# Chunk 0 of a DeltaNet layer in two halves of 32 tokens, in front of an MLP that fills TensorE

## The chip, the cores and the metric

The kernel runs on one core of one Trainium2 chip. The metric is the time of one execution on the device, in microseconds. TensorE (PE) multiplies matrices, VectorE (DVE), ScalarE (ACT) and GpSimd (POOL) do the elementwise work, and SyncE (SP) issues DMAs; ACT and POOL issue DMAs too. Everything is in 32-bit floats.

## The reference

Two layers, one after the other. The first is a DeltaNet recurrence for 4 batches, 8 heads, 768 tokens and a head size of 48; the second a layer norm and an MLP with a residual, on rows of 384.

```python
k_n = k / (np.linalg.norm(k, axis=-1, keepdims=True) + 1e-06)
for t in range(S):
    kt, vt, bt = (k_n[:, :, t], v[:, :, t], beta[:, :, t, None])
    y[:, :, t] = np.einsum('bhd,bhde->bhe', q[:, :, t], state)
    v_old = np.einsum('bhde,bhd->bhe', state, kt)
    state = state + bt[:, :, :, None] * np.einsum('bhd,bhe->bhde', kt, vt - v_old)
...
x = y.transpose(0, 2, 1, 3).reshape(B, S, H * D)
xn = (x - mu) / np.sqrt(var + 1e-06) * g_ln
out = x + np.maximum(xn @ w_ch1, 0.0) @ w_ch2
```

## The kernel before

**Chunks.** The 768 tokens are cut into 12 chunks of 64. Inside a chunk the recurrence becomes products of small matrices: the Gram matrix G of the keys, its scaled lower triangle, the inverse of one plus that triangle (one 64x64 matrix for each of the 32 batch and head pairs), u (the corrected values, from the inverse and v), the masked products P of queries and keys, the outputs y = P u plus the queries on the state, and the state's update. Then each chunk's 256 rows (4 batches of 64 tokens) go through the layer norm and the MLP.

**Three ways to the inverse.** Chunk 0 has nothing ahead of it, so its inverse is on the way of everything. It is made by doubling blocks, in `first_inverse` (line 648): at level n blocks of 2^n rows are joined. Each level has a product E (line 722), a predicated copy under a mask (731), a product Z (741), transposes on DVE (687) that give the natural form, and copies on ACT (681) that give the turned form. Chunk 0 needs five levels of products after a beginning, for two groups `g` of 8 heads each; a product is 16 matrix products of 64x64, in four quarters of the array, and each is two PE instructions. Chunks 1 to 11 use `rows_inverse` (826): the Gram matrix goes to DRAM and comes back with one 32x32 block in each partition, and DVE eliminates row by row, 31 steps of a multiplication (860) and a subtraction (867). The result is stored, loaded into `xt`, and `join` (883) joins two blocks of 32 into 64. The first call, ri1 below, is for chunk 1 alone, the second, ri2, for chunks 2 and 3, the third, ri4, for chunks 4 and 5.

**Chunk 0's rows.** Partitions hold a pair of batches of 64 tokens each (`half(e)`), and the second pair lies beside it. `first_beta` turns beta on PE, `first_norms` takes the norms of the keys, `first_swaps` moves the norms to the other half of the partitions, and `recur(0, ...)` makes u, y, the layer norm and the state. MLP 0 is done by halves of 128 rows in `by_halves` (1317): w1 in 12 blocks f (1326), relu on ACT (1334), w2 in 12 blocks (1341). The later MLPs run in blocks of 256 rows (1300) or in forms with fewer products (1221, 1423).

**Weights.** The MLP's weights come in 12 pieces of 768 KB, 0 to 5 for w1 and 6 to 11 for w2. Each is fetched by a DMA on ACT's queue into one of five buffers (`fetch`), converted by two steps on ACT (524, 532) and one on DVE (529), and added on POOL (542). A buffer is free for the next piece when its sum is done.

**Order.** All work is put down as steps by `add`; the numbers in `ORDER` then say in which order they are given out. Each engine does its own steps in exactly that order (`in_this_order`), so a step that waits holds back all later steps of its engine, DMA issues on its queue included. "z" in the list is a product of zeros on PE. The arguments `due`, `t0`, `pr`, `cap` and the costs have no effect: `Line.add` drops them.

Of the kernel before, what the change touches and what calls it, by code (L numbers as in the profile page):

```python
# [63 lines left out]
155 243 148 238 151 236 332 152 225 675 156 z 215 157 240 159 158 214 237 239 160 216 162 161 257 46 241 168 164 166 333 206 165 334 245 207 417 163  # L64
# [136 lines left out]
def kernel(  # L201
# [240 lines left out]
    def nat(src, c, e):  # L442
        return src[2 * e : 2 * e + 2, :, c * C : (c + 1) * C, :].rearrange("g h p d -> p (g h) d")
# [1209 lines left out]
```

## Time and profile before

| | |
|---|---|
| time, median of 3 runs | 507.94 us (506.93 to 510.24) |
| span of the profiled execution | 508.8 us; its own time is not listed apart from it |
| PE busy | 488.6 us, 96% |
| DVE, ACT, POOL busy | 353.8, 249.0, 275.6 us |
| first product of MLP 0 | 54.46 us |
| mean granted clock of PE | 0.965 |

The span runs from the first to the last instruction. A line of the timeline has the start, the time that a run of like instructions took, the engine, the line of the kernel, what was written from what, partitions and elements, and how many; in brackets stands how long the engine was idle just before, and what ended that. "Issue" there means that the engine waited for nothing that the profile shows. A granted clock of 0.50 means that PE ran at half speed.

### The profile page before, as it was taken

The numbers are of one execution on the slowest core, as the hardware profiler recorded it, in microseconds if no ns is written. First come the engines' busy times: TensorE is split into PE (matmuls) and PEld (weight loads), VectorE is DVE, ScalarE is ACT, GpSimd is POOL, SyncE is SP. The second block draws the span as 40 slices with busy tenths as digits, with TensorE's granted clock in tenths as the row PEclk, the third lists the DMA queues.
The fourth block names the chain that finished last, engine by engine and source line by source line (L and its number), as shares of the span: only waits on it lengthen the run. The fifth ranks groups of instructions, "written<-read, shape, count | busy, mean of one in ns | idle before, by whom it ended". The sixth has DMA issues, their size and how long they took to land.

```text
span 508.8 us, 22190 instructions
## 1 busy us (share of the span) xinstructions
PE 488.6 (96%) x9606; PEld 447.6 (88%) x9606; DVE 353.8 (70%) x780; ACT 249.0 (49%) x620; POOL 275.6 (54%) x430
## 2 busy tenths in 40 slices
PE   7778999999899999999999999999999999999996
PEld 3667988788788898899999999999999999999996
DVE  9668987997679648896649898568899328143251
ACT  5758873643544524627435535435563257363230
POOL 5464537264755496438894363492543850645633
PEclk9756799999999999999999999999999999999999
DMA  8988796667656566546834434766154402211101
GB/s 168 293 160 190 249 200 85 98 152 130 90 86 87 187 119 119 65 99 149 194 58 62 94 62 135 150 94 97 50 92 106 111 20 45 60 48 46 24 18 31
DMA packets 196097, 54.99 MB, mean 108 GB/s; under 512 B 186076, under 2 KB 189404, under 8 KB 196000
## 3 DMA queue, kind: packets, MB, share of 16 engines
q1 hardware_dynamic: 189920, 40.58, 41.9%
q10 hardware_dynamic: 3872, 9.83, 6.0%
q0 software_dynamic: 2208, 3.17, 3.8%
q8 instruction: 75, 1.23, 1.0%
q14 instruction: 22, 0.18, 0.1%
HBM read 36.64 MB, written 16.91 MB: 105 GB/s over the span
## 4 chain that ended last, share of the span: by engine, by line
PE 90%; DVE 5%; issue 2%; POOL 1%; DMA 1%; SPq 0%; ACT 0%; DVEq 0%; POOLq 0%; ACTq 0%
PE f L1423 29%; PE f L1221 22%; PE f L1300 9%; PE f L1326 4%; PE f L1341 3%; PE by L983 2%; PE by L1024 2%; PE two L983 2%; PE by L775 2%; PE two L1017 2%; PE two L775 2%; PE two L1034 2%; PE f L775 1%; DMA xt<-xd 1%; PE by L741 1%
## 5 line engine op out<-in xcount | busy, mean ns | idle before, releaser
L1410 POOL TENSOR_TENSOR h_all<-h_all 128x256 f32<-128x256 f32 x123 | 89.9, 742 | 135.1 <-PE f L1423 121.3
L1423 PE MATMUL f<-w_sb,h_all 128*128 128x192 f32 x492 | 109.8, 332 | 1.6 <-DVE rstd L967 1.6
L1423 PEld LDWEIGHTS f<-w_sb,h_all 128*128 128x128 f32 x492 | 81.8, 190 | 3.6 <-issue 1.9
L1423 PE MATMUL f<-words,h_all 128*128 128x192 f32 x396 | 84.5, 330 | 0.3 <-POOL h_all L1410 0.3
L860 DVE TENSOR_TENSOR tmp<-xb,gb 128x87 f32<-128x87 f32 (+21 forms) x186 | 73.7, 396 | 4.9
L867 DVE TENSOR_TENSOR xb<-xb,tmp 128x87 f32<-128x87 f32 (+21 forms) x186 | 73.6, 396 | 4.8
L1241 DVE TENSOR_TENSOR h_all<-h_all,f 128x512 f32<-128x512 f32 x96 | 63.5, 682 | 14.3 <-PE f L1221 13.2
L1423 PEld LDWEIGHTS f<-words,h_all 128*128 128x128 f32 x396 | 66.6, 190 | 1.7 <-POOL h_all L1410 1.0
L1300 PE MATMUL f<-xnt,w_sb 128*128 128x256 f32 x216 | 50.2, 382 | 0.0
L349 POOL DMA_DIRECT2D tb<-in_k_dram x64 | 42.0, 660 | 10.3 <-DVE kt L755 9.4
L1243 ACT ACTIVATE h_all<-h_all 128x512 f32<-128x512 f32 x48 | 28.5, 624 | 34.6 <-DVE h_all L1241 34.3
L1300 PEld LDWEIGHTS f<-xnt,w_sb 128*128 128x128 f32 x216 | 40.2, 190 | 5.3
L1237 ACT COPY h_all<-f 128x512 f32<-128x512 f32 x48 | 26.2, 590 | 34.3 <-PE f L1221 17.4
L1441 DVE TENSOR_TENSOR o<-f,x 128x192 f32<-128x192 f32 x33 | 11.6, 352 | 38.9 <-PE f L1423 22.3
L1221 PE MATMUL f<-words,w_sb 128*128 128x128 f32 x256 | 31.7, 276 | 0.0
L1309 ACT ACTIVATE h_all<-f 128x256 f32<-128x256 f32 x36 | 13.3, 382 | 35.1 <-PE f L1300 34.9
L1221 PEld LDWEIGHTS f<-words,w_sb 128*128 128x128 f32 x256 | 30.0, 192 | 0.2
L1221 PE MATMUL f<-xnt,w_sb 128*128 128x128 f32 x192 | 25.4, 276 | 0.0
L542 POOL TENSOR_TENSOR w_sb<-words 128x768 uint32<-128x768 uint32 (+1 forms) x11 | 15.0, 1365 | 17.7 <-DVE words L529 13.3
L1221 PEld LDWEIGHTS f<-xnt,w_sb 128*128 128x128 f32 x192 | 23.7, 192 | 0.1
L1326 PEld LDWEIGHTS f<-xnt,w_sb 128*128 128x128 f32 x144 | 19.2, 200 | 3.3 <-issue 0.2
L1088 ACT ACTIVATE xnt<-xnt,g_sb 128x256 f32<-128x256 f32 x27 | 12.5, 498 | 19.2 <-DMA xnt<-xld 19.1
(246 smaller groups left out, 958.4 us busy)
## 6 DMA issues: line engine op xcount, KB each, us to landing
words<-in_moe_w_ch_dram ACTq DMA_DIRECT2D x10, 768.0 KB, 5.2
gd<-gsb SPq DMA_DIRECT2D x11, 512.0 KB, 3.6
v<-in_v_dram SPq DMA_DIRECT2D x24, 192.0 KB, 4.3
kr<-in_k_dram SPq DMA_DIRECT2D x46, 96.0 KB, 3.6
out_dram<-o SPq DMA_DIRECT2D x44, 96.0 KB, 2.8
xld<-xlt SPq DMA_DIRECT2D x9, 384.0 KB, 3.3
xnt<-xld SPq DMA_DIRECT2D x36, 96.0 KB, 3.2
gb<-gd SPq DMA_DIRECT2D x44, 64.0 KB, 3.0
```

Of the source, the lines that this page charges most:

```text
L349: add(eng, cost, lambda: QUEUE[eng].dma_start(out=out_, in_=in_), r, w, bulk=n * ns / 16e3, **kw)
L775: nc.tensor.matmul(pair[hp][half(e ^ (hp & n)), (g * NP + j) * C : (g * NP + j + 1) * C], kt[drows(hp), l], rt[drows(hp), i],)
L860: lambda j=j, n=n, w=w, t=t: nc.vector.tensor_tensor(out=t, in0=xv[:, 0:n, j : j + 1].to_broadcast([np_, n, w]), in1=gv[:, j : j + 1, j + ...
L867: "DVE", dve(n * w), lambda t=t, rest=rest: nc.vector.tensor_tensor(out=rest, in0=rest, in1=t, op=ALU.subtract),
L1221: nc.tensor.matmul(wide(p[:, 128 * n : 128 * n + 128]), w[n // 2][:, n % 2 * 128 : n % 2 * 128 + 128], r, start=start and n == 0, stop=Tru ...
L1237: add("ACT", act(512), lambda: nc.scalar.copy(o, p), pk, ok)
L1241: add("DVE", dve(512), lambda: nc.vector.tensor_tensor(out=o, in0=o, in1=p, op=op), pk, ok)
L1243: add("ACT", act(512), lambda: nc.scalar.activation(o, o, ACTF.Relu), [], ok)
L1300: nc.tensor.matmul(p[:, 0:TOK], w1_sb[:, t, f * 128 : (f + 1) * 128], xnt[:, t], start=(t == 0), stop=(t == KC - 1))
L1326: nc.tensor.matmul(p[:, 0:128], w1_sb[:, t, f * 128 : (f + 1) * 128], xnt[:, t, cols], start=(t == 0), stop=(t == KC - 1))
L1410: add(eng, cost, lambda: e.tensor_tensor(out=out_, in0=x, in1=y, op=op), r, w, port=2 if eng == "Pool" else 1, pr=-2)
L1423: lambda f=f, t=start and f == 0: nc.tensor.matmul(p[:, 0:D2], lhs(f), rhs[:, f], start=t, stop=(f == F2 - 1), skip_group_check=True),
```

## The change

Chunk 0 is cut into two halves of 32 tokens. Half `g` holds tokens 32g to 32g + 31 of all four batches, with 32 partitions for each batch (`quad(b)`) and the heads side by side. Chunk 1 and all later ones are computed as before.

- The loads of k, q and v for chunk 0 become eight of 32 tokens each (`load_first`), k on SP and ACT, q and v on SP; beta comes in four rows of loads, and DVE turns it (`btok`). `first_swaps` is gone.
- `first_inverse(g, ...)` makes the 32x32 inverses of one half, in four levels. The scaled Gram matrices of two batches are set beside zeros as blocks of 64, so that E and Z are each 8 products of 128x64 by 64 columns. The turned form is brought back by four copies on ACT, the natural form by two transposes on DVE.
- Half 0 goes through u, y and the layer norm by itself. For half 1, `first_between` keeps the products of its keys with half 0's; they take half 0's u off the values (w0), and its y has a term from each half (y0x, y0).
- The state after chunk 0 is made in two parts (`first_state`), with two products for each block, one from each half.
- In the MLP by halves, a half is now 32 tokens of four batches; its outputs are stored by four DMAs for each half, for two before.
- Masks and begin matrices are fewer and lie in other tiles.
- `ORDER` is new from end to end: 3016 steps for 2997, and two "z" for one.

The core of the diff, without the order:

```diff
+    def load_first(src, dst, keys, engs, g, **kw):
+        for b in range(4):
+            dma(
+                engs[b % len(engs)], dst[quad(b), g * H : g * H + H, 0:D],
+                src[b, :, g * BK : g * BK + BK, :].rearrange("h t d -> t h d"), H * BK, 16.5, [], keys(b, g), **kw,
+            )
...
+    def first_beta(**kw):
+        add("DVE", 0.23, lambda: nc.vector.transpose(btok, brow), [("brow", b) for b in range(4)] + ["brow0"], ["btok"], **kw)
...
+    def first_between(pair, **kw):
+        for hp in range(2):
+            v, dst = parts_of(pair, hp, 0)[:, :, 1], pts[0][:, hp : H : 2]
...
+    def first_inverse(g, pair, E, Z, **kw):
...
+        for n in range(1, LAST + 1):
...
+            def prod_e():
                 for j in range(NP):
+                    for hp in range(2):
+                        nc.tensor.matmul(
+                            ebank[half(hp), j * C : j * C + C], gs[:, 2 * j + hp], xn[:, 2 * j + hp].rearrange("p e t -> p (e t)")
+                        )
+            pe(16, prod_e, [("g", 0, g), ("qt", 1, g, 0), ("qt", 1, g, 1)], ek, 0.43, name=f"E{n}{g}", **kw)
...
+            def prod_z(ep=ep):
+                for j in range(NP):
+                    for e in range(2):
                         nc.tensor.matmul(
+                            zbank[half(e), j * C : j * C + C], ep[:, 2 * j + e], xt[:, j, e].rearrange("p n t -> p (n t)")
                         )
+            pe(16, prod_z, [ekey, *xtk], zk, 0.43, name=f"Z{n}{g}", **kw)
+            z = heads_of(zbank)
+            if n < LAST:
+                nat(z, zk)
+                back(z, zk, n)
+            else:
+                add("ACT", act(256), lambda: nc.scalar.copy(done, z), zk, [("done", g)], **kw)
...
+        def first_u(g, ps, pk):
+            xd, p_u = dones[:, heads2[g]], ps[:, 0:DM].rearrange("p (h d) -> p h d", d=D)
+
+            def prod_u():
+                for h in range(H):
+                    for b in range(4):
+                        nc.tensor.matmul(p_u[quad(b), h], xd[quad(b), h], vv[quad(b), g * H + h])
...
+        if not c:
+            for g in range(2):
...
+                if g:
+                    p_w = first_half(0, pu, uk, [(pts[0][:, 0:H], 0)], [("pt", 0, 0), ("u", 0)], "w0")
...
+                first_u(g, pu, uk)
+                if g:
+                    first_half(0, py, yk, [(pts[1][:, H:GH], 0)], [("pt", 1, 1), ("u", 0)], "y0x")
+                first_half(g, py, yk, [(pts[1 - g][:, heads2[g]], g)], [("pt", 1 - g, g), ("u", g)], f"y0{g}")
...
+                ln_act(0, x, kw, (g,))
+                turn_x(g, pu, uk)
+            for b in range(2):
+                first_state(b)
+            return
...
-            for e in range(2):
+            for b in range(4) if not c else ():
+                dma("SP", out[b, g * BK : g * BK + BK], os_[g][quad(b)], BK, 105, o_keys(g), [("out", c, g, b)], pr=-5)
```

What each engine does, in the new order, around the start of MLP 0 (names as above; "f" and "w2" are the MLP's blocks):

- PE: E3 and Z3 of half 0, then Z1 of half 1, E4 of half 0, P of half 0, E2 of half 1, Z4 of half 0, Z2 of half 1, u of half 0, E3 of half 1, y of half 0, Z3 of half 1, P of half 1, the transpose of half 0's rows, E4 of half 1, f0, f1, w0, Z4 of half 1, f2, a transpose for chunk 2's keys, f4, the other one, u of half 1, f6, f3, f8, y0x, y0, G of chunk 2, ... the join of chunk 1 follows block 5 of half 1's w2.
- DVE: the last predicated copy of half 1, a mask of P, and only then ri1's 31 row steps, with the conversions of pieces 6 to 8 and 11 and half 1's steps among them. Before, ri1 began between levels 3 and 4.
- ACT: the scalings of half 0's rows, a conversion step of piece 6, the first relu, the other step of piece 6, the fetch of piece 8, a step of piece 7, the next two relus.
- SP: k, then chunk 1's k, q and v of chunk 0, chunk 1's Gram matrix out and back. Later: two reads for ri2, ri1's result out, six more reads for ri2, one load of q, then the four loads of ri1's result.

More of the change, by code (lines that the diff above doesn't have):

```diff
@@ L389 @@
     )
-    MASKED = (0, 1, 2, 3, 4, 5)
+    MASKED = (0, 1, 2, 3, 4)
     for n in MASKED:
@@ L453, in load_v @@
         for e in range(2):
-            dma("SP", vs[c % NV][half(e)], nat(v, c, e), GH * C, 16.5, w=[("v", c % NV, e)], **kw)
+            dma(
+                "SP", vs[c % NV][half(e)], nat(v, c, e), GH * C, 16.5, w=[("v", c % NV, e)],
+                after=[("v", 0, 2 * e + b, g) for b in range(2) for g in range(2)] if c == 2 else (), **kw,
+            )
     def load_raw(c, engs=("SP", "SP"), dst=None, keys=None, **kw):
@@ L618, in scale_v, with first_v @@
+    def first_v(g, **kw):
+        vg, kg = vs[0][:, heads2[g]], knrm[0][:, heads2[g], None].to_broadcast([128, H, D])
+        add(
+            "Pool", 0.8, lambda: nc.gpsimd.tensor_tensor(out=vg, in0=vg, in1=kg, op=ALU.mult),
+            [("kn", 0, g)], [("v", 0, b, g) for b in range(4)], **kw,
+        )
     def scale_v(c, kn, kk, **kw):
@@ new lines, in parts_of, with first_p @@
+    def parts_of(pair, hp, g):
+        return pair[hp][:, 0 : NP * C * (2 - g)].rearrange("p (j g t) -> p j g t", j=NP, t=C)
+    def first_p(g, pair, **kw):
+        first_products(qts[0], "qt", g, pair, f"P0{g}", **kw)
+        for hp in range(2):
+            v, dst = parts_of(pair, hp, g), pts[1 - g].rearrange("p (g j n) t -> p g j n t", g=2, n=2)[:, g:, :, hp].rearrange("p g j t -> p j g t")
+            mask = both[:, None, 0 : 2 - g].to_broadcast([128, NP, 2 - g, C])
+            add(
+                "DVE", dve(256 * (2 - g)), lambda v=v, dst=dst, mask=mask: nc.vector.tensor_tensor(out=dst, in0=v, in1=mask, op=ALU.mult),
+                pair[2 + hp] + ["own", "pown"], [("pt", 1 - g, n) for n in range(g, 2)], **kw,
+            )
@@ L706, in first_inverse @@
                 ),
-                [("g", 0, g), ("mask", 0)], bk, port=1, **kw,
+                [*ek, ("mask", n)], [ekey], **kw,
             )
-            add(
-                "DVE", dve(512), lambda i=i: nc.vector.transpose(xnj_[:, :, i], begin[:, :, i]), bk,
-                [("qt", 1, g, n) for n in range(2)], **kw,
-            )
-            back(g, lambda n, r, i=i: begin[r, n, i], [bk, bk])
-        for n in range(1, 6):
-            ep, ekey = paired(BEGIN[n][0]), tuple(BEGIN[n][1:])
-            for g in range(2):
-                E, i = next(turns), half_g[g]
-                def prod_e(i=i, E=E, n=n):
-                    for j, hp, e in order:
-                        a = half(e ^ hp)
+            def prod_z(ep=ep):
+                for j in range(NP):
+                    for e in range(2):
@@ L809, in queries @@
                 ),
-                pk + ["pmask"], [("pt", one_of(c))], after=[("pt", 1, g) for g in range(2)] if c == 1 else (), **kw,
+                pk + ["pmask"], [("pt", one_of(c))], after=[("pt", one_of(c), g) for g in range(2)] if c < 3 else (), **kw,
             )
@@ L918, in join, with raw_keys0 @@
             )
+    def raw_keys0(g):
+        return [("kr", 0, b, g) for b in range(4)] + [("krpad", 0)]
     def raw_keys(c):
@@ L937, in norms, with ln_act @@
         scale_v(c, knrm[i], kk, **kw)
-    def ln_act(c, x, kw):
+    def ln_act(c, x, kw, parts=(0, 1)):
         i = c % 2
-        for g in range(2):
+        for g in parts:
             ck = [("ln", i, g)]
@@ L969, in ln_act @@
                 add("ACT", act(384), lambda g=g, rs=rs: nc.scalar.mul(xlns[g], xlns[g], rs), ck, [("xln", g)], **kw)
+    SK = [("s_all", b) for b in range(2)]
     def recur(c, pr, lag=0.0):
@@ new lines, in first_half, with prod @@
+        def first_half(g, ps, pk, terms, keys, name):
+            p_ = ps[:, 0:DM].rearrange("p (h d) -> p h d", d=D)
+            def prod():
+                for n, (lhs, g0) in enumerate(terms):
+                    for h in range(H):
+                        for e in range(2):
+                            nc.tensor.matmul(
+                                p_[half(e), h], lhs[half(e), h], us[half(e), g0 * H + h],
+                                start=(g == 0 and n == 0 and h == 0), stop=(g == 1 or n == len(terms) - 1), skip_group_check=True,
+                            )
+            pe(32 * len(terms), prod, keys, pk, 0.64 * len(terms), name=name, **kp_e)
+            return p_
@@ L1019, in recur, with turn_x, turn, out_y @@
             add("ACT", act(768), lambda: nc.scalar.copy(u_j, p_2), TWO, [("u", 0), ("u", 1)], **kw)
-        def out_y(js, p_y=p_y):
-            for j in js:
+        xnt = xnts[c % 2]
+        unbegun = [("begin", g) for g in range(2)] if c == 1 else ()
+        def turn_x(g, tp=None, bk=None):
+            tp, bk = (by[:, g], BY[2 * g : 2 * g + 2]) if c else (tp, bk)
+            def turn():
+                for t in range(KC):
+                    nc.tensor.transpose(tp[:, t * 128 : (t + 1) * 128], xlns[g][:, t * 128 : (t + 1) * 128], ident)
+            add("PE", 0.33, turn, [("xln", g), "ident"], bk, np=3, arr=0.33, **kp_e)
+            if g > c:
+                add(
+                    "DVE", dve(384),
+                    lambda: nc.vector.tensor_tensor(
+                        out=xnt[:, :, g * 128 : (g + 1) * 128], in0=tp[:, 0:DM].rearrange("p (t n) -> p t n", t=KC),
+                        in1=g_sb[:, :, None].to_broadcast([128, KC, 128]), op=ALU.mult,
+                    ),
+                    bk + ["g_sb"], [("xnt", c % 2, g, t) for t in range(KC)], after=unbegun, **kw,
+                )
+                return
+            for t in range(KC):
+                add(
+                    "ACT", act(128),
+                    lambda t=t: nc.scalar.mul(
+                        xnt[:, t, g * 128 : (g + 1) * 128], tp[:, t * 128 : (t + 1) * 128], g_sb[:, t : t + 1]
+                    ),
+                    bk + ["g_sb"], [("xnt", c % 2, g, t)], after=unbegun, **kw,
+                )
+        def out_y():
+            for j in range(GP):
                 for hp, e in hp_e:
+                    a = half(e ^ hp)
                     nc.tensor.matmul(
-                        p_y[half(e), hp, j], pt[half(e ^ hp), 2 * j + hp], us[half(e ^ hp), 2 * j + hp],
-                        start=(c == 0 and j == js[0]), stop=True, skip_group_check=True,
+                        p_y[half(e), hp, j], pt[a, 2 * j + hp], us[a, 2 * j + hp], start=False, stop=True, skip_group_check=True,
                     )
@@ L1036, in state_up, with first_state, prod_s @@
                     )
+        def first_state(b):
+            ps, pk = ((p_2, TWO), (p_y, BY))[b]
+            def prod_s():
+                for j in range(NP):
+                    for hp, e in hp_e:
+                        a = quad(2 * e + b)
+                        for g in range(2):
+                            h0 = g * H + 2 * j + hp
+                            nc.tensor.matmul(
+                                ps[DP * hp : DP * hp + DP, e, j], kp[a, h0 * DP : h0 * DP + DP], us[a, h0],
+                                start=(g == 0), stop=(g == 1), skip_group_check=True,
+                            )
+            rk = raw_keys0(0) + raw_keys0(1)
+            add("PE", 0.8, prod_s, rk + [("u", 0), ("u", 1)], pk, np=64, arr=0.32, name=f"s0{b}", pr=-40, lag=lag)
+            add(
+                "ACT", act(384), lambda: nc.scalar.copy(s_all[:, :, b * NP : b * NP + NP], ps[:, :, 0:NP]), pk, [("s_all", b)], pr=-40,
+            )
         def up(**kw):
@@ new lines, in up, with y_copy @@
+            add("DVE", dve(768), lambda: nc.vector.tensor_tensor(out=s_all, in0=s_all, in1=p_2, op=ALU.add), TWO, SK, **kw)
+        y_j = x.rearrange("p g (j n d) -> p g n j d", n=2, d=D)
+        def y_copy(g):
+            add(
+                "ACT", act(384), lambda: nc.scalar.activation(
+                    y_j[:, g], p_y[:, :, g * NP : g * NP + NP], ACTF.Copy, accum_out=st[:, c % 2, g, 0:1]
+                ),
+                BY, [("x", c % 2, g), ("ln", c % 2, g)], **kw,
+            )
@@ L1152, in sums_of_w1 @@
     def sums_of_w1(last):
-        gone = [(n, 1, *x) for n in ("qt", "pt") for x in ((), *((g, *y) for g in range(2) for y in ((), (0,), (1,))))]
+        gone = [("done", g) for g in range(2)] + [(n, 1, *x) for n in ("qt", "pt") for x in ((), *((g, *y) for g in range(2) for y in ((), (0,), (1,))))]
         sub, plus, both = ALU.subtract, ALU.add, (0, 1)
@@ L1353, in by_halves @@
                 pk + [("x", 0, g), ("ln", 0, g)], o_keys(g), pr=-5,
+                after=["nought", "xor", "bits", "eye", *[("mask", n) for n in MASKED]],
             )
@@ L1495 @@
     chain = dict(pr=-100)
-    load_raw(0, ("SP", "ACT"), **chain)
+    add("Pool", 0.1, lambda: nc.gpsimd.memset(brow, 0.0), [], ["brow0"], pr=-100)
+    raw0 = kraws[0].rearrange("p (h d) -> p h d", d=DP)
+    load_first(k, raw0, lambda b, g: [("kr", 0, b, g)], ("SP", "ACT"), 0, **chain)
+    for b in range(4):
+        dma("Pool", brow[BK * b : BK * b + H], beta[b, :, 0:C], H, 20, ["brow0"], [("brow", b)], **chain)
+    load_first(k, raw0, lambda b, g: [("kr", 0, b, g)], ("SP", "ACT"), 1, **chain)
     load_raw(1, pr=-100)
```

402 lines of the change are left out of this document (179 added, 223 removed), and 167 rows, old and new, of the table ORDER.

## The prediction

> **What bounds the kernel now.** I read the page's totals first, then the busy time by stretches, then the first 130 us engine by engine, with what each waited for.
>
> ```profile
> span 508.8 us, 22190 instructions
> PE 488.6 (96%) x9606; PEld 447.6 (88%) x9606; DVE 353.8 (70%) x780; ACT 249.0 (49%) x620; POOL 275.6 (54%) x430
> ```
> TensorE is busy for all but 20.2 us. The stretches (PE, PEld, DVE, ACT, POOL, then granted clock, DMA share, GB/s) show where:
>
> ```profile
> 10.00:20.00 10.00, 6.94 (x203) 5.84 (x202) 7.36 (x20) 7.91 (x21) 0.90 (x2) 0.77 1.11 305
> 30.00:40.00 10.00, 7.48 (x213) 6.44 (x211) 5.88 (x21) 4.69 (x14) 4.98 (x6) 0.50 0.82 152
> 60.00:70.00 10.00, 9.91 (x209) 8.77 (x201) 9.35 (x23) 6.95 (x19) 4.54 (x6) 1.00 0.94 239
> 110.00:120.00 10.00, 10.00 (x103) 8.63 (x106) 9.40 (x20) 2.34 (x7) 4.70 (x7) 1.00 0.35 96
> 120.00:140.00 20.00, 18.28 (x349) 16.28 (x342) 11.88 (x23) 9.70 (x30) 13.95 (x21) 1.00 0.74 98
> ```
> Up to 50 us PE idles about 13 us and runs at half clock. From 54 us it is full, but for some 2.5 us between 137 and 144 and the last tail. So only what moves the start of the saturated part, adds PE work behind it, or makes new stalls there can move the end. DVE is over 90% full from 60 to 120 us: the row inverses of chunk 1 (ri1) and of chunks 2 and 3 (ri2). The marks of this part in the PE timeline:
>
> ```profile
> 13.46 0.69 PE L722 MATMUL two<-qt,gsb 64*64 64x64 f32 x32 [0.18 <-DVE qt L710]
> 18.90 1.97 PE L568 MATMUL f<-ident,tb 128*128 128x128 f32 x8
> 32.06 1.08 PE L722 MATMUL by<-qt,gsb 64*64 64x32 f32 x32
> 36.20 0.59 PE L741 MATMUL by<-xt,xt 64*64 64x64 f32 x11 [1.53 <-issue]
> 46.37 1.65 PE L1000 MATMUL two<-v,xt 64*64 64x48 f32 x32
> 54.46 2.52 PE L1326 MATMUL f<-xnt,w_sb 128*128 128x128 f32 x12
> 86.19 0.75 PE L898 MATMUL f<-xnj,gsb 32*32 32x32 f32 x64
> 104.48 2.75 PE L1300 MATMUL f<-xnt,w_sb 128*128 128x256 f32 x12
> 124.90 0.75 PE L898 MATMUL f<-xnj,gsb 32*32 32x32 f32 x64
> ```
> In order: level 1 of chunk 0's inverse, a transpose at half clock, level 4, u of the first half (46.37), the start of MLP 0 (54.46), join of chunk 1 (86.19), MLP 1 (104.48), join of chunk 2 (124.90). I call the start of MLP 0 **T**.
>
> **Part 1: the start of chunk 0.** The order lists were read by numbering the add calls; each engine's sequence follows. On POOL four beta rows replace two, and the fourth stands behind a 0.95 us clear, two half clears, the identity, g_sb and one k block. By rows (DMA issue 0.62 to 0.72, clear 0.95) it is issued near 7.9 us and lands 3.4 later (median of the beta loads), at 11.3. Behind the DVE instruction that waits for it are queued the scale, both halves of the scaled Gram matrix, the masked begin and its transposes: ten small ones at 0.15 to 0.23, two of 0.40, two of 0.45, two of 0.43, 4.4 us. Level 1 begins near 15.8, not 13.46: **+2.3**. One k load sits behind an ACT copy and lands near 8, in that cover. The sixteen q and v loads on SP (0.63 each, 10 us) replace four of 3.6 us together; SP waited 8.2 us there for the Gram copy, which hides them.
>
> **Part 2: four levels for five.** Before, five levels with both groups took 13.46 to 46.1, 6.5 each. Now half 0 goes ahead and half 1 trails. A product is 16 instructions of 64 columns on 128x64 tiles, a shape the trace lacks. Bounds: 0.69 us (32 of 64x64 at full clock) and 1.97 (eight transposes of 128 columns at half clock, if the two column halves don't overlap). I take 1.05: two halves of 16 have the columns of four quarters of 32, and those took 1.08 at half clock. A level is then E 1.05, predicated copy 0.71, Z 1.05, two transposes 0.86, some 0.4 of handovers: 4.1. Following the new lists, level 3 waits about 1.9 us for four ACT copies that stand behind weight conversions of 0.55 each, and level 4 waits 2.8 us on PE for P of half 0 (32 of 128 columns, 1.75) and E2 of half 1. Four levels: 20.7, so 36.5, against 46.1.
>
> **Part 3: from the inverse to T.** Copy of the finished inverse 0.4, then Z2 of half 1 on PE, u at 37.5. From u to T took 54.46 - 46.37 = 8.1. The chain is the same (u, scale, y, copy, mean, centre, transpose, three scalings); four products of half 1 fill the gaps that the last Z and G2 filled. T = 45.6, **8.9 earlier**. Doubt: the four PE gaps marked "issue" before (5.1 us together) may come three times; but I priced PE at half clock throughout, where two stretches ran at full. I give T 40 to 51.
>
> **Part 4: PE work that now lies behind T.** At full clock, per instruction 0.017 (64 in 1.08): correction of half 1 (w0, 32) 0.54; last Z of half 1 0.45; kt2 transposes 0.9; u of half 1 (64) 1.08; y of half 1 in two terms 1.08 against 0.65; G2 1.09; the state in two parts of 64 for one of 64, +1.08. Sum **+5.6**. Before, u of half 1, kt2 and G2 lay ahead of or at T. Were PE alone the limit, the end would move -8.9 + 5.6 = -3.3.
> A change of tile size costs: in the saturated part an interval of 0.33 grows to 0.42 ahead of the 32x32 products at 187 us, and the next group takes 0.59, not 0.49. That is 0.1 each way; six more changes, +0.6. The Trainium skill, TensorEngine Tiling (Array Packing), section Key Properties, says that changing the tiling mode drains TensorE; the row agrees and sets its size.
>
> **Part 5: what is late next.** The old list starts ri1's 62 steps at 41.8, inside the inverse's waits:
>
> ```profile
> 41.81 0.14 DVE L860 TENSOR_TENSOR tmp<-xb,gb 64x31 f32<-64x31 f32 x1
> 73.80 0.51 SPq L349 DMA_DIRECT2D xd<-xb  x1
> 78.46 2.08 SPq L349 DMA_DIRECT2D xt<-xd  x4
> 85.35 0.70 DVE L888 STREAM_TRANSPOSE xnj<-xt 128x512 f32<-128x512 f32 x1
> ```
> The new list puts them behind half 1's last predicated copy, at T + 1. They took 24.1 us (L860 12.91 + L867 11.20); 4.9 of other steps lie among them (four conversions at 0.55, w0's subtraction, u, centre, xnt, mask). End: T + 30 = 75.6, later than the 72.5 of before. Then store, six reads of ri2 and one q load on SP at 0.6, loads, landings, ri2's scaling, transpose: 13.7 us before (72.5 to 86.2). Two reads already stand ahead of the store now; I take 11.5: join 1 at T + 41.5 = 87.1. PE's own list reaches it after 37.2 us of work, at 82.8 to 84. So it stalls 3 to 4 us, and the gain of part 4 is gone.
> From join 1 the chain to MLP 1 is 16.2 (e to z 2.4, to u 2.4, to y 2.2, y 1.1, norm 5.5, transpose and scale 2.6) over 13.6 us of PE work. MLP 1: 87.1 + 16.2 = 103.3, with G5 (1.1) still to do: 104.4 against 104.48, -0.1.
> ri2 starts at T + 40.5 and has 22.9 of its own and 9.8 of others among it (6.5 before), 33.5 with gaps: 119.6 against 115.3. Store to join 2 took 9.6: 129.2, with 3.3 us more products done than at 124.9: +1.0. Before lost 2.4 near 138 to 144 (1.6 at DVE rstd, 0.8 at issue); the new list's join 3 stands about 1.3 short: -1.1. The eight output stores of chunk 0 (four before, 0.5 each) are +2 us on SP, partly ahead of ri2's loads; its cover is this stall, and I charge nothing. From 160 us on the PE work is the same, and PE has no idle time there.
>
> **Sum.** -0.1 + 1.1 - 1.1 is -0.1; the 0.6 of tile changes falls into the stalls ahead of the joins. The span stays 508.8 - 0.1 = 508.7. The runs shown have median 507.94, 0.9 below that span, so the time is **508 us**. Its own bounds come from T (-4.5 to +4.5 around 45.6) and 2 for the stalls: 503 to 513.
>
> **Rivals.**
> (a) *The start comes earlier and everything follows.* The PE clock was 1.00 from 22.5 to 25.5 and from 43.5 to 45. If it stays so through the inverse, eight products save 0.4 each, P 0.9, u 0.6, two products of half 1 0.8: 5.5 us, T = 40, end 502.5; with join 1's data 1.5 sooner, 501. For it: less queued on DVE, and fewer issue gaps. Against it: PE has 256 product instructions for 640, so it is idle more, and with 640 it already ran at 0.50 from 30 to 42. The Trainium skill, TensorE: Matmul & The Clock Gate, Terms and Part 1, says an idle window of about 3.4 us halves the clock; the rows agree in direction, and by it this rival is the less likely.
> (b) *The first relu waits for weights; slower.* ACT's new list has the conversion of piece 6 ahead of the first relu and piece 7 ahead of the second. Piece 6 can be fetched only when piece 3 has been added by POOL (near 35). Fetches land in 5.2 us at the median: 41, in time. But DMA was 0.82 to 1.11 busy in these stretches, and T's 8.9 us ask for the same bytes sooner. From a landing after 46 each microsecond stops the two relu banks, PE behind them, and on DVE ri1 behind the conversion of piece 6. A landing in 11 to 12 us adds 6: 514.
> (c) *The 128x64 products cost twice; slower.* At the upper bound 1.97, eight on the chain of half 0 add 7.4, and part is hidden by conversions: T near 52, end 514.5. For it: no row shows the shape. Against it: the 64x64 quarters do overlap.
> (d) *PE alone limits.* If ri1 and its loads keep up, -3.3 + 0.6: 505. MLP by halves exists already, so the words of the change promise nothing more there.
>
> **How the numbers follow.** Forecast 0.34, (d) 0.08, (a) 0.27, (b) 0.17, (c) 0.14. A measurement of this kernel tells about 1%, 5 us, from no change. (a) is faster by over 1%; forecast and (d) are within, less 0.01 on the slow edge; (b) and (c) are over it. So 0.27 faster, 0.41 same, 0.32 slower. The range reaches to (a) and past (b) and (c) by their 2 us: 500 to 517; the likeliest case's own is 503 to 513.
>
> **What would show it.** Right: level 1 near 16, four levels of 4 to 6 us, MLP 0 from 43 to 48, ri1 ending later than 72 us, a PE wait of 2 to 5 us ahead of the join of chunk 1, and MLP 1 near 104. Wrong: MLP 0 by 41 (a); PE waiting on ACT relu behind a words DMA after T (b); products of 1.9 us (c); no wait at join 1 (d). A forecast within 1% that comes from T at 45.6 with losses elsewhere than at join 1 would be right by accident.

## The result, and the profile after

The changed kernel takes 536.69 us (median of 4 runs, 534.01 to 538.66), the kernel before, measured beside it, 507.84: a ratio of 1.0554, 95% interval 1.0514 to 1.0594. The forecast was 508, its range 500 to 517; the kernel got 28.9 us slower. The times and ratios of the experiments below come from four chips, on each of which the kernel before took 507.6 to 509.4 us beside them. The page's totals of the kernel after:

```profile
span 534.5 us, 21792 instructions
...
PE 500.2 (94%) x9408; PEld 451.6 (84%) x9408; DVE 361.6 (68%) x778; ACT 248.6 (47%) x616; POOL 277.6 (52%) x438
```

PE idles 34.3 us instead of 20.2, and it is busy for 11.6 us more. The stretches of the kernel after (PE, PEld, DVE, ACT, POOL, then granted clock, DMA share, GB/s) show both:

```profile
20.00:40.00 20.00, 11.71 (x234) 9.42 (x228) 10.93 (x28) 15.52 (x41) 11.74 (x19) 0.80 0.57 167
...
50.00:60.00 10.00, 3.45 (x41) 3.01 (x32) 6.83 (x17) 3.15 (x10) 1.47 (x1) 0.80 0.80 159
...
60.00:80.00 20.00, 18.44 (x389) 16.84 (x388) 14.53 (x33) 12.78 (x31) 7.00 (x7) 0.93 0.59 173
...
100.00:120.00 20.00, 17.21 (x424) 12.90 (x425) 17.13 (x43) 10.13 (x31) 9.56 (x15) 0.91 0.62 83
...
120.00:140.00 20.00, 19.34 (x269) 16.37 (x268) 17.23 (x42) 7.54 (x21) 6.79 (x12) 1.00 0.49 124
```

From 50 to 60 us, where MLP 0 was to be under way, PE works 3.45 us of 10. The same marks in the PE timeline as before the change:

```profile
18.90 0.69 PE L737 MATMUL f<-qt,gsb 128*64 128x64 f32 x16
...
40.57 1.07 PE L754 MATMUL f<-xt,xt 128*64 128x64 f32 x16
...
43.09 1.50 PE L1017 MATMUL f<-v,q_last 32*32 32x48 f32 x64
...
50.08 0.55 PE L1058 MATMUL f<-ident,xln 128*128 128x128 f32 x3
...
57.87 2.93 PE L1392 MATMUL f<-xnt,w_sb 128*128 128x128 f32 x12 [6.37 <-ACT xnt L1073]
...
104.60 0.75 PE L911 MATMUL f<-xnj,gsb 32*32 32x32 f32 x64 [0.36 <-DVE xnj L901]
...
123.36 1.56 PE L1366 MATMUL f<-xnt,w_sb 128*128 128x256 f32 x6 [0.66 <-ACT xnt L1073]
...
148.77 0.75 PE L911 MATMUL f<-xnj,gsb 32*32 32x32 f32 x64
...
165.59 1.15 PE L1001 MATMUL two<-s_all,kt 48*64 48x48 f32 x64
```

They are: level 1 of half 0 (18.90, predicted 15.8), the last product of its level 4, its u (43.09, predicted 37.5), the turn of x, the start of MLP 0 (T = 57.87, predicted 45.6), join of chunk 1, MLP 1, join of chunk 2, and the first sums of chunk 3. The inverse ends earlier than before, but PE waits 6.37 us for ACT ahead of MLP 0. With T and the sums of chunk 3 as cuts, the loss divides so (us; the sums of chunk 3 began at 149.25 before):

| stretch of PE's timeline | before | after | more |
|---|---|---|---|
| start to T | 54.46 | 57.87 | 3.4 |
| T to the first sums of chunk 3 | 94.8 | 107.7 | 12.9 |
| from there to PE's last product | 355.3 | 365.3 | 10.0 |

These are two single executions; the stretches add up to 26.3 us, the medians differ by 28.9. The forecast for the three stretches was 8.9 less, some 8.8 more, and nothing.

### The profile page after: what moved, and what is told of

The parts are those of the page before. It is cut to its first block, busy times and chain, and to the rows that moved or that the text cites. A ratio compares the mean times of both kernels' runs of the same rounds, so it can differ in the third digit from the quotient of the medians.

```text
span 534.5 us, 21792 instructions
## 1 busy us (share of the span) xinstructions
PE 500.2 (94%) x9408; PEld 451.6 (84%) x9408; DVE 361.6 (68%) x778; ACT 248.6 (47%) x616; POOL 277.6 (52%) x438
## 4 chain that ended last, share of the span: by engine, by line
PE 71%; DVE 10%; SPq 4%; DMA 4%; ACT 2%; issue 1%; ACTq 0%; DVEq 0%
PE f L1492 27%; PE f L1287 21%; PE f L1366 4%; DVE xb L880 4%; SPq L343 4%; DVE tmp L873 3%; PE by L1001 2%; PE by L1083 2%; PE two L1046 2%; PE f L1392 2%; PE two L1001 2%; PE by L788 1%; PE two L1092 1%; PE two L788 1%; DMA tb<-in_q_dram 1%
## 5 line engine op out<-in xcount | busy, mean ns | idle before, releaser
L1492 PE MATMUL f<-w_sb,h_all 128*128 128x192 f32 x492 | 94.4, 330 | 0.8 <-ACT h_all L1375 0.8
L1492 PEld LDWEIGHTS f<-w_sb,h_all 128*128 128x128 f32 x492 | 79.9, 190 | 2.1 <-ACT h_all L1375 0.9
L873 DVE TENSOR_TENSOR tmp<-xb,gb 128x87 f32<-128x87 f32 (+21 forms) x186 | 78.0, 419 | 5.2
L880 DVE TENSOR_TENSOR xb<-xb,tmp 128x87 f32<-128x87 f32 (+21 forms) x186 | 77.4, 416 | 4.8
L1492 PE MATMUL f<-words,h_all 128*128 128x192 f32 x396 | 77.5, 332 | 0.3 <-issue 0.3
L1492 PEld LDWEIGHTS f<-words,h_all 128*128 128x128 f32 x396 | 64.8, 190 | 1.8 <-issue 0.4
L1366 PEld LDWEIGHTS f<-xnt,w_sb 128*128 128x128 f32 x216 | 39.7, 190 | 7.6 <-DVE words L1510 1.4
L1510 DVE TENSOR_TENSOR o<-f,x 128x192 f32<-128x192 f32 x33 | 11.3, 351 | 46.0 <-PE f L1492 42.4
L1287 PE MATMUL f<-words,w_sb 128*128 128x128 f32 x256 | 32.9, 278 | 0.0
L1392 PE MATMUL f<-xnt,w_sb 128*128 128x128 f32 x144 | 20.9, 294 | 6.4 <-ACT xnt L1073 6.4
L1392 PEld LDWEIGHTS f<-xnt,w_sb 128*128 128x128 f32 x144 | 18.8, 203 | 8.2 <-ACT xnt L1073 6.5
L1287 PE MATMUL f<-xnt,w_sb 128*128 128x128 f32 x192 | 25.6, 278 | 0.0
L1287 PEld LDWEIGHTS f<-xnt,w_sb 128*128 128x128 f32 x192 | 23.4, 192 | 0.3
```

The costliest lines, as they stand in the source:

```text
L873: lambda j=j, n=n, w=w, t=t: nc.vector.tensor_tensor(out=t, in0=xv[:, 0:n, j : j + 1].to_broadcast([np_, n, w]), in1=gv[:, j : j + 1, j + ...
L880: "DVE", dve(n * w), lambda t=t, rest=rest: nc.vector.tensor_tensor(out=rest, in0=rest, in1=t, op=ALU.subtract),
L1287: nc.tensor.matmul(wide(p[:, 128 * n : 128 * n + 128]), w[n // 2][:, n % 2 * 128 : n % 2 * 128 + 128], r, start=start and n == 0, stop=Tru ...
L1366: nc.tensor.matmul(p[:, 0:TOK], w1_sb[:, t, f * 128 : (f + 1) * 128], xnt[:, t], start=(t == 0), stop=(t == KC - 1))
L1392: nc.tensor.matmul(p[:, 0:128], w1_sb[:, t, f * 128 : (f + 1) * 128], xnt[:, t, cols], start=(t == 0), stop=(t == KC - 1))
L1492: lambda f=f, t=start and f == 0: nc.tensor.matmul(p[:, 0:D2], lhs(f), rhs[:, f], start=t, stop=(f == F2 - 1), skip_group_check=True),
```

## Why MLP 0 starts late: two experiments that change no engine's program

What holds ACT ahead of the three scalings that make xnt? Its timeline and SP's, in the kernel after:

```profile
44.56 0.39 ACTq L343 DMA_DIRECT2D words<-in_moe_w_ch_dram  x1
...
50.84 0.42 ACT L703 COPY xt<-by 64x64 f32<-64x64 f32 x2 [0.54 <-DVE qt L708]
...
56.10 0.38 ACTq L343 DMA_DIRECT2D words<-in_moe_w_ch_dram  x1
...
56.59 0.37 ACT L1073 ACTIVATE xnt<-f,g_sb 128x128 f32<-128x128 f32 x1 [5.32 <-DMA tb<-in_q_dram]
...
41.48 8.00 SPq L343 DMA_DIRECT2D beta_b<-in_beta_dram  x2
...
50.93 0.59 SPq L343 DMA_DIRECT2D tb<-in_q_dram  x1
...
52.28 0.60 SPq L343 DMA_DIRECT2D tb<-in_q_dram  x1
```

ACT has nothing to compute from 51.3 on; in its queue the *issue* of fetch 7 (weights, 56.10) stands ahead of the scalings and waits. The profile names a load of q as the releaser, which has nothing to do with weights. In the program, all 424 DMAs of SP and ACT use eight semaphores (DMAHW0 to 7) in turn, in the order of the list over both queues. A semaphore here is a counter that a DMA raises when it has landed and on which an instruction can wait. Fetch 7 (first line) waits for one of them besides its buffer, and the last issue before it that uses the same one is the load of q on SP (second line), eight issues earlier:

```
L343 DMACopy words_68<-in_moe_w_ch_dram 128x2x768 [waits DMAHW1_49,Pool_49]
L343 DMACopy tb_70<-in_q_dram 64x16x48 [waits DMAHW1_49]
```

So in this program an issue waits until the eighth issue before it has landed, whoever issued it. The load of q was itself late: on SP, beta_b6's eighth predecessor was fetch 6, issued at 44.56, and SP stood until 49.5. The reading can be tried without touching any engine's program, since only the order *between* the two queues decides who is eighth. **First** (396 is fetch 6, 401 fetch 7, 428 and 434 are beta_b0 and beta_b6, 437 the late load of q):

```diff
-396 199 256 368 369 341 343 83 84 354 85 428 434 342 344 436 431 437 356 355 440 430 429 353 435 203 ... 401
+396 199 256 368 369 203 ... 401 341 343 83 84 354 85 428 434 342 344 436 431 437 356 355 440 430 429 353 435
```

> The kernel after, with twenty DMA issues of SP (from the keys of chunk 2 to beta_b7) written behind fetch 7 in the list of steps; the instructions of every engine and their order on it are unchanged. Theory 1 (a DMA issue on SP or ACT waits until the eighth issue before it, both queues counted together, has landed): fetch 7's eighth predecessor is now fetch 5, long landed, so fetch 7 issues at about 50.9 us instead of 56.1 and the first product of MLP 0 starts at 52 to 53 instead of 57.87. beta_b6 on SP, whose eighth predecessor is now fetch 7 instead of fetch 6, waits until about 56 instead of 49.5, so the keys of chunk 2 come 6 us later and PE, which turns them some 4 us into MLP 0, may lose part of it again: time 531 to 536. Rival (fetch 7 waits for its buffer, or for a place in ACT's own queue, which are as before): fetch 7 at 56.1, start of MLP 0 at 57.9, 536.7 within 1.

Measured: 539.07 us, ratio 1.0593 (1.0541 to 1.0646). Fetch 7 goes at 48.49 and MLP 0 starts at 50.26, 7.6 us earlier, and on SP beta_b0 and beta_b6 wait for fetches 6 and 7, to 53.6 (expected 56). But the hold has moved, where I had not looked: fetch 8's eighth predecessor is now the same load of q, and ACT's copies of half 1 stand behind fetch 8. Timelines of ACT, SP and PE in this run:

```profile
48.49 0.39 ACTq L343 DMA_DIRECT2D words<-in_moe_w_ch_dram  x1
...
60.89 0.38 ACTq L343 DMA_DIRECT2D words<-in_moe_w_ch_dram  x1
...
47.81 5.74 SPq L343 DMA_DIRECT2D beta_b<-in_beta_dram  x2
...
57.08 0.60 SPq L343 DMA_DIRECT2D tb<-in_q_dram  x1
...
50.26 2.93 PE L1392 MATMUL f<-xnt,w_sb 128*128 128x128 f32 x12 [1.16 <-ACT xnt L1073]
...
61.57 1.12 PE L754 MATMUL by<-xt,xt 128*64 128x64 f32 x16 [7.19 <-ACT xt L703]
```

PE loses 7.19 us there instead of 6.37 at T, so the time is above the 531 to 536 expected. That the buffer or ACT's own queue held fetch 7 is refuted; that an earlier T is an earlier end is refuted too. **Second**, fourteen of the SP issues ahead of fetch 6 and six behind fetch 7, so that no late transfer is eighth before anything here:

```diff
-396 199 256 368 369 341 343 83 ... 437 356 355 440 430 429 353 435 203 ... 401
+341 343 83 ... 437 356 396 199 256 368 369 203 ... 401 355 440 430 429 353 435
```

> The kernel after, with fourteen of the same twenty SP issues written ahead of fetch 6 and the last six behind fetch 7; again the instructions of every engine and their order on it are unchanged. Theory 1 (eighth issue back must have landed): nothing in this stretch has a late eighth predecessor any more: beta_b6 goes at about 41.5 instead of 49.5, fetch 7 at about 51 instead of 56.1, MLP 0 starts at 52 (after 57.87), and the time falls by what the start gains, 5 to 6 us, to 531. Theory 2 (the start of MLP 0 does not set the end, the chain of the inverse of chunk 1 does): MLP 0 starts at 52 but join 1 stays near 104.6 and the time at 536. Rival (buffers or the queues themselves hold them): nothing moves, 536.7 within 1.

Measured: 529.65 us, ratio 1.0409 (1.0358 to 1.0460), 7.0 us less than the kernel after and 9.4 less than the first variant, with the same instructions in the same order on every engine. From its ACT, SP and PE timelines:

```profile
48.80 0.39 ACTq L343 DMA_DIRECT2D words<-in_moe_w_ch_dram  x1
...
40.46 1.29 SPq L343 DMA_DIRECT2D beta_b<-in_beta_dram  x2
...
50.56 1.60 PE L1392 MATMUL f<-xnt,w_sb 128*128 128x128 f32 x12 [1.21 <-ACT xnt L1073]
...
58.27 1.62 PE L1392 MATMUL f<-xnt,w_sb 128*128 128x128 f32 x6 [3.13 <-ACT h_all L1400]
```

Both issues of beta_b now take 1.29 us, T is 50.6, and PE's 6.37 us at T are gone; 3.13 at a relu are new (below). Join 1 moved by 3.7 us, to 100.86, and the time by 7.0, so theory 2 is refuted. The Trainium skill, DMA: Bandwidth & Descriptors, section "Why a DMA increments its semaphore by 16 and not by 1", asks for one semaphore for each transfer in flight, since a wait can pass too early where two share one. No run here shows stale data; these show the other side, what eight slots handed round in turn cost when one holder is slow.

## The start, and the weights in ACT's queue

In the kernel after, level 1 starts 3.1 us later than predicted. G of half 0 needs both copies of kt, which I had not seen, and the second stands on ACT behind fetch 2, the squares of half 1 and fetch 1:

```profile
10.78 0.38 ACTq L343 DMA_DIRECT2D words<-in_moe_w_ch_dram  x1
...
11.26 0.52 ACT L611 ACTIVATE xln<-kr 128x384 f32<-128x384 f32 x1 [2.68 <-DMA tb<-in_q_dram]
...
11.69 0.59 ACT L593 COPY kt<-by 128x512 f32<-128x512 f32 x1
```

ACT idles 2.68 us there until a load of q has landed, and in the program that load is the eighth issue before fetch 2: the wait that holds T stands here too. A second load of ACT's function table (1.28 us) is there as well, since the square root is no longer ACT's first activation. The first mend:

```diff
(SP)  -66 65 59 61 64 63                   +59 61 66 65 64 63
(ACT) -35 100 30 102 96 88 109 87 97 ... 49   +49 35 100 30 102 96 88 87 97 109
(DVE) the sum of squares of half 1 (110) behind half 0's scale (106)
```

> The kernel after, with the first 12 us mended: the two SP loads of half 1's keys go ahead of chunk 1's, the square root of eps is ACT's first activation again, and the squares, sums and roots of half 1 stand behind the second copy of kt and half 0's scaling. Theory: one table load less on ACT (1.28 us), the second kt copy at about 9.5 instead of 11.69, the first products of G at about 10 instead of 12.33, E of level 1 at 16 to 17 instead of 18.90; but fetch 7 still waits for the load of q issued on SP, whose own place hangs on fetch 6, so the start of MLP 0 moves less, 0 to 2.5 us: time 534 to 537. Rival (the whole chain moves with its start): MLP 0 starts 2.5 earlier and the time is 534.

Measured: 536.76 us, ratio 1.0550 (1.0509 to 1.0591): no gain. One table load is gone, but level 1 is at 18.68: fetches 2 and 1 still stood ahead of the second copy, and left at 11.20 and 11.62. On the split order, with these two moved behind as well:

```diff
(ACT) -102 96 88 87 97 109 ... 111         +102 96 97 109 ... 111 88 87
```

> On the split order of issues (529.65 us, start of MLP 0 at 50.6): the first 12 us mended as in e2, and besides fetches 2 and 1 on ACT stand behind the second copy of kt and the squares and root of half 1, because in e2 both copies waited behind these two issues until 12.1. Theory (the late first product of level 1 is ACT's queue): second kt copy at 9 to 9.5, E of level 1 at 15 to 16 (17.7), MLP 0 at 48 to 49, time 527 to 528. Rival (the levels wait for DVE and for loads that come when they did): MLP 0 at 50.6 and 529.7 within 1.

Measured: 528.49 us, ratio 1.0373 (1.0350 to 1.0396). Level 1 starts at 14.32, as the theory said, but T is 50.84. Its PE and ACT timelines:

```profile
14.32 0.69 PE L737 MATMUL f<-qt,gsb 128*64 128x64 f32 x16 [0.82 <-DVE tmp L619]
...
19.54 1.11 PE L754 MATMUL f<-xt,gsb 128*64 128x64 f32 x14 [3.33 <-ACT xt L703]
...
18.32 0.54 ACT L552 ACTIVATE words<-words 128x384 uint32<-128x384 uint32 x1 [3.88 <-DMA words<-in_moe_w_ch_dram]
...
18.87 0.61 ACT L703 COPY xt<-xnt 64x128 f32<-64x128 f32 x2
```

ACT's first weight conversion stands between the copies of level 1 and waits 3.88 us for its weights; the copies behind it hold PE 3.33 us. An earlier inverse meets weights that come when they came. In the split order the relu, too, stood behind a conversion that waited:

```diff
-402 608 606    +608 606 402        (relus f2, f1 ahead of conversion 7)
```

> On the split order of issues (529.65): the first two relus behind f1 and f2 of MLP 0 go ahead of the first part of conversion 7 on ACT, which in that run waits for fetch 7's data until 56.9 and holds PE for 3.1 us. Nothing else moves. Theory (each us that PE idles or does not idle before 100 us is a us of the end, since PE is full behind): PE's wait of 3.1 us shrinks to under 1 and the time is 527 to 528. Rival (PE meets the same late weights or keys some steps later): the wait comes back at another product, 529.7 within 1.

Measured: 528.26 us, ratio 1.0353 (1.0316 to 1.0390), and PE's wait of 3.13 us is gone: the gain is smaller than expected, and within the error of the split order (level 1 began 1.1 us later in the profiled execution, at 18.8). Last, all of these together and the conversions of fetch 2 behind levels 0 and 1:

```diff
(ACT) 233 231 90 243 245 behind 146 (the last copy of level 1)
(DVE) 232 244 behind 151 (the predicated copy of level 2)
```

> On the split order with the mended start and the two relus ahead: the weight conversions of fetch 2 (five steps on ACT, two on DVE, with the issue of fetch 4) go behind the copies of levels 0 and 1 of the first half, because in the run with the mended start E of level 1 was at 14.3, but ACT's first conversion waited for its weights until 18.3 and held the copies, and PE's Z of level 1 waited 3.3 us. Theory (the inverse waits for weights in ACT's queue, not for its own chain): Z of level 1 whole at 16 to 17, MLP 0 at 47.5 (50.8), time 524 to 526. Rival (the next weight step in the queue, or DVE, holds it again): MLP 0 at 50 to 51, 527 to 528.5.

Measured: 526.53 us, ratio 1.0373 (1.0350 to 1.0396). Z of level 1 is whole at 16.29, T 49.29. By ratios these three variants can't be told apart, and they lie 0.3 to 0.5% under the split order, with intervals that overlap with its own. Of 3.0 us won at the start of level 1 (17.7 to 14.7), 1.3 are left at T: PE now waits 2.3, 1.8 and 2.7 us for transposes on DVE (qt), which has conversions among them. So the queue of weights around the inverse is worth 2 to 3 us at most; the traces show its waits, the times do not settle it.

## The later part: changes of tile size

From the first sums of chunk 3 on, the kernel after needs 10.0 us more on a PE that is full in both. Its work there is 1.1 us more by counting products, its idle time 1.7 more. A tile size is the part of PE's array that a product takes, 128x128, 64x64 or 32x32 for example; 48 rows or columns take 64. Counted so in the traces, PE changes between tile sizes 145 times there, against 104. To price that I pulled the small products of the kernel *before* apart, at 25 places like this one (chunk 4's sums qs4 and ks4, an MLP step of the neighbourhood between):

```diff
-m2 p3 0 | qs4 | ks4 | m2 p2 5
+m2 p3 0 | qs4 | m2 p2 5 | ks4
```

> The kernel before with PE's order alone changed from the first sums of chunk 3 on: wherever two small products stand next to each other, one step of the MLP goes between them (25 places, each step moved past one small product). Changes between tile sizes rise from 110 to 147 there, about what the kernel after has (145). Theory (a change costs about 0.2 us where PE is full, by the fit over the traces): 37 times 0.2 to 0.227 is 7.4 to 8.4 us more, about 516. Rival (the changes cost nothing; what the kernel after loses behind chunk 3 has another cause): 508.7 within 1.5. Between: by the regrouped kernel, which won some 2 us by 16 fewer, 0.13 a change, 513.

Measured: 518.1 us, ratio 1.0202 (1.0177 to 1.0228), 10.5 us more. In its trace the part behind chunk 3's first sums takes 364.6 us instead of 355.3; 1.8 of the 9.3 are idle. The changes there rise from 104 to 148, by 44 and not by the 37 of the text above, and 7.5 over 44 is 0.17 each. The place itself, first before, then pulled apart:

```profile
178.94 0.49 PE L1423 MATMUL f<-w_sb,h_all 128*128 128x192 f32 x2
179.36 1.15 PE L983 MATMUL by<-s_all,qt 48*64 48x48 f32 x64
180.33 1.11 PE L983 MATMUL two<-s_all,kt 48*64 48x48 f32 x64
181.37 0.59 PE L1423 MATMUL f<-words,h_all 128*128 128x192 f32 x2
181.80 0.49 PE L1423 MATMUL f<-w_sb,h_all 128*128 128x192 f32 x2
```

```profile
177.74 0.49 PE L1423 MATMUL f<-w_sb,h_all 128*128 128x192 f32 x2
178.16 1.15 PE L983 MATMUL by<-s_all,qt 48*64 48x48 f32 x64
179.24 0.59 PE L1423 MATMUL f<-words,h_all 128*128 128x192 f32 x2
179.76 1.15 PE L983 MATMUL two<-s_all,kt 48*64 48x48 f32 x64
180.84 0.59 PE L1423 MATMUL f<-w_sb,h_all 128*128 128x192 f32 x2
181.27 0.49 PE L1423 MATMUL f<-words,h_all 128*128 128x192 f32 x2
```

Before, the group takes 2.86 us from first to last start, and the MLP step is 0.33 where MLP steps follow one another: 3.19. Pulled apart it takes 3.53. Two more changes, 0.34, so 0.17 each at this place too. For the kernel after, 41 more changes times 0.17 is 7.0 of the 10.0 us, with 1.7 idle and 1.1 of work 9.8. That this price holds for its changes is carried over, not shown by a run of its own.

The reverse did not pay. On the split order, small products put next to each other again, for instance `-1251 1091 ... 1252` `+1251 1252 1091` (ks4, qs4):

> On the split order of issues (529.65): PE's order alone is changed; in chunks 2 to 11, where the dependences allow it, the product of state and queries is put next to that of state and keys (same tile size), and the state update next to y. Changes between tile sizes on PE go from 220 to 194 over the kernel, from 145 to 121 from chunk 3 on. Theory (fitted from the traces so far: a change of tile size costs 0.227 us where PE is full, and 27 more of them are 6 of the 10 us that the kernel after loses from chunk 3 to the end): minus 26 times 0.227, 5.9 us, to 523.7 (522.5 to 525.5, less what PE then waits for the moved steps' inputs). Rival (the changes cost nothing, the late loss is carried over from the start): 529.7 within 1.5.

Measured: 533.06 us, ratio 1.0467 (1.0442 to 1.0492), slower. Behind chunk 3's first sums PE idles 6.3 us instead of 1.9, in new waits for DVE, and its busy time falls by 2.2 us, 0.09 for each of 24 changes: half the price of adding one, and why is open. All together:

> The split order, the mended start, the two relus and the regrouped products together. Theory (the terms add up on a PE that is full behind 60 us: 2, 2.5 and 5.9 off 529.65): 519 to 520. Rival (each only moves a wait that another then shows): 524 to 527. Either way slower than before at 508.7; what is left over is idle time inside the inverse and changes of tile size.

Measured: 531.41 us, ratio 1.0438 (1.0411 to 1.0465): the terms do not add; the regrouped order's waits (6.2 us idle) stay and eat the others. The other way to win the changes back is the order of the kernel before for all later steps, first on the kernel after, then on the one cleared on ACT:

> The kernel after up to the middle of MLP 0 (650 of its 3018 steps, about 110 us), and from there its remaining steps in the order that the kernel before has them. By PE work ahead, the kernel after is some 18 us behind at the first sums of chunk 3 and 26 behind at the end. Theory (the new order of the later steps costs by itself, by more changes between tile sizes on PE and small waits): 5 to 8 us come back, time 529 to 532. Rival (the later loss is only carried over from the late start): 536.7 within 1.5.

> The kernel cleared on ACT (526.53 us) up to the middle of MLP 0, and from there the remaining steps in the order of the kernel before, as in e5: changes of tile size fall from 220 to 187. Theory (0.2 us a change where PE is full): 33 times 0.2 is 6.6 off, 520. Rival (an order that was fitted to an earlier join meets late joins here, as in e5, where 5.7 us of new idle time took the gain): 526 to 530. A version faster than before (508) is in neither.

Measured: 539.54 us (median of the three runs behind the ratio), ratio 1.0611 (1.0517 to 1.0706), and 534.55, ratio 1.0517 (1.0447 to 1.0587). The first is not faster than the kernel after, the second 1.4% slower than the one cleared on ACT. In the later part the changes are 104 again, and PE's busy time does fall, from 363.3 to 357.3 us and from 363.2 to 360.8; but PE idles 6.0 and 6.5 us there. More is lost ahead of it: from T to chunk 3's first sums, where the two orders meet, they take 114.7 and 112.5 us instead of 107.7 and 105.7. Some of PE's waits in the second, by what it waited for (us in total, times, longest):

```profile
PE f L911 <- DVE xnj L901: 3.0, 2, 2.6
...
PE f L911 <- issue: 2.7, 1, 2.7
...
PE f L1366 <- issue: 1.9, 1, 1.9
...
PE two L1001 <- issue: 1.6, 1, 1.6
```

The first is a join that comes later than that order was written for, ahead of chunk 3's sums. The other three have no releaser in the profile; they stand behind the sums and are 6.2 of the 6.5 us idle there. No variant comes near the kernel before.

## The prediction, step by step

- **Part 1, level 1 at 15.8: wrong, 18.90.** The queue on DVE was read rightly, the one on ACT not: G of half 0 needs the second kt copy, which stands behind a fetch whose issue waits 2.68 us. With ACT mended it is 14.32, below my figure: DVE's transpose of beta went at 9.81, not 11.3.
- **Part 2, a product at 1.05 and four levels at 20.7: the price right, the sum short.** A product of 16 takes 0.69 us at a granted clock of 1.00 (18.90) and 1.12 at 0.50 (26.18); rival (c) is refuted. From level 1 to u it took 24.2 us for 21.7: PE idles 8.7 us there in nine waits, most of it for ACT's copies (xt) and DVE's transposes (qt), where the sum had two waits of 4.7. Its own terms add up to 21.1, not 20.7. The product shown at 32.06 in the timeline of before is the second of level 3, not level 4, and ri1 began there (41.81) between levels 4 and 5; neither moves the sum.
- **Part 3, u to T 8.1: wrong, 14.8; this is the step that failed by most.** The step put the wait of a DMA *issue* at nothing: I followed what each DMA moves and needs, and not what its issue waits for. ACT waited 5.32 us in fetch 7's issue. With only the order between the queues changed, u to T is 50.56 - 42.30 = 8.3, as forecast. T came out 12.3 late: 3.1 from part 1, 2.5 from part 2, 6.7 here. In the trace of before SP waited 4.5 us in all for weights, which I did not follow up.
- **Part 4, +5.6 of PE work behind T: right in kind.** Counted by products, at the interval that like products have at full clock, work ahead of T falls by 3.8 and work from T to chunk 3 rises by 3.9. Since T was not early, this is loss. **Six more changes of tile size at 0.1: the term that was mis-sized.** They are 51 over the whole list (214 against 163), 41 of them behind chunk 3's first sums, at 0.17 by the kernel pulled apart.
- **Part 5, ri1 ends at T + 30: T + 31.6, but by luck.** It began 4.0 us ahead of T, not 1 behind it, and took 35.6 us instead of 29, with a wait of 3.4 for a weight conversion on ACT among them. In the trace of before its last step ends at 73.7, not 72.5. **A stall of 3 to 4 us at join 1: wrong.** PE waits 0.36 there. Join 1 comes at T + 46.7, not 41.5, and PE's own way to it was as long: 43.9 us busy, not 37.2, and 2.8 in small waits. From T to 63 us the granted clock was 0.51 (the first twelve products took 2.93 us, 1.60 in the split order), and there are 16 changes of tile size up to the first sums of chunk 1, against 9. **"From 160 us on the PE work is the same"** was right in products, but for 1.1 us, and wrong in time, by 10.
- **Rivals.** (a) came in part in its condition, not in its effect: the granted clock was 0.80 from 20 to 40 us, against 0.59 before, but T was held by the waits above. (b) came in kind and in the size of its wait, 7.0 us for the 6 given, by another mechanism: the weights had a place to land, but their issue waited, and PE stood at xnt instead of the first relu. Its time, 514, did not come. (d) was not reached: idle time and changes of tile size both grew.

Of the 12.9 us from T to chunk 3's sums, 3.9 are work and 3.5 idle time (6.1 against 2.6). The granted clock of 0.93 and 0.91 in two stretches gives an estimate of 18.44 x 0.07 + 17.21 x 0.09 = 2.8. Close to 3 are open; changes of tile size don't explain them, for there are 44 in this stretch, against 43. Open as well is why the kernel cleared on ACT still stays 3.7% above before: 9.1 us of that are the later part; for the rest I have only the work behind T and a sum of small waits.

## What to carry to other kernels

An instruction that issues a DMA can wait for a transfer it has nothing to do with; in a list written over several queues, look which earlier issue each shares its semaphore with, and keep slow transfers from standing that far ahead of an engine that computes. An order that is moved as a whole changes more than the stage it was moved for: count the changes of tile size over the full list, times a price from the trace, before believing that the later part is the same. Bringing a chain forward helps only as far as every queue it passes, here the weight conversions on ACT and DVE, is brought forward with it.

## What the hardware showed that I had not expected

- PE stops in the midst of like products with no releaser in the profile, for up to 2.7 us: after 39 of 64 small products, 25 follow later. In the two runs with the late order of before, the stops fall on the same products (1.62 and 1.61, 2.50 and 2.66 us). They come to 5.9 us in the kernel before, 1.2 after, and 3.6 in the one pulled apart. Counted in PE's instructions, weight loads included, neighbouring stops of a run stand 256 apart or a multiple of it, to within one record (in the kernel before 256, 257, 256 and 17 times 256), and the remainder of the position by 256 is the same, 193 or 194, for all 35 such stops of the thirteen traces. So the place follows from the position in PE's list. Why only a few of these positions stop PE was not tried.
- A change of tile size added to a full PE costs 0.17 us, at the place shown and on the mean of 44, not the 0.1 that one interval had suggested. Taken out of the split order, 24 changes saved 0.09 each.
